# A recurrent attention and feed-forward kernel: inputs of three batches in half-batch loads from ScalarE's queue

## Chip, core and metric

One core of a Trainium2 chip runs the kernel. The engines are named as in the profile: PE (matrix multiplies; PEld is its weight load), DVE (vector), ACT (scalar and activation functions), POOL, and SP, which here only issues DMAs. Each engine works through its own instructions in program order and waits at the first one whose inputs or buffers are not ready. A DMA is issued by SP or ACT on that engine's queue. The metric is device time in microseconds of one execution, as a median over runs; details come from one profiled execution.

## What is computed

Four batches, eight heads, 768 steps, head size 48. A gated linear recurrence gives `y`; a feed-forward block with the gate `h * cos(h)` follows.

```python
for t in range(S):
    state = alpha[:, :, t, :, None] * state + np.einsum('bhd,bhe->bhde', k[:, :, t], v[:, :, t])
    y[:, :, t] = np.einsum('bhd,bhde->bhe', q[:, :, t], state)
x = y.transpose(0, 2, 1, 3).reshape(B * S, H * D)      # 3072 x 384
h = x @ w_in                                           # w_in 384 x 2048
g = h * np.cos(h)
out = g @ w_out                                        # w_out 2048 x 384
```

## The kernel before

The 3072 rows are cut into 24 chunks of 128 steps; chunk j belongs to batch j // 6 and holds all eight heads. In a chunk the recurrence is done as matrix products: cumulated logarithms of alpha give scale factors, k and q are scaled by them, k·q scores are masked, and a state is carried from chunk to chunk of a batch. The feed-forward block of a chunk has two halves of eight 128-column blocks.

The whole program is a hand-scheduled list: `ORDER` is a string of units, each a letter and a number, and every engine executes its instructions in the order in which the units stand there. The units that matter, with the engine:

- `a`, `k`, `q`, `v` + chunk: load of one input. In the kernel before SP issues one load of 192 KB for each chunk and tensor (lines 100 and 104), 96 in all. A row of one head is 48 floats, so each load is cut into 1024 pieces of 192 bytes. Buffers: six chunks for k, q, v (`PF`), four pairs of chunks for alpha.
- `z0`..`z3`, `Z0`..`Z3`: a quarter of `w_in` (line 111) or `w_out` (line 124), 768 KB each, from SP. `r`, `s` cast a quarter of `w_in` (DVE two thirds, ACT one third); `R` casts a quarter of `w_out` (DVE for even numbers, ACT for odd ones).
- `i`/`l`: logarithm of alpha on ACT for one or two chunks (line 144); `c`/`C`: cumulated sums on PE (lines 157, 161); `d`/`E`: two exponentials on ACT (lines 175, 177). Logarithm and exponential use one activation table and the cosine another, so ACT loads a table at each change (lines 137 and 338).
- `K`, `Q`: scaled k and q on POOL (lines 185, 191; `Q0` and `Q1` on DVE); `b`: cast of v on POOL (line 195); `E_`: a small factor on POOL (line 200).
- `T`: transpose of scaled k and q; on PE with a copy `t` by DVE (lines 218, 224) for chunks below `TD`, from there as a DMA transpose issued by SP (line 211).
- `A`, `m`: scores on PE, mask on DVE (lines 235, 244). `S`, `u`: state on PE and its update on DVE and POOL (lines 260, 272, 274). `Y`, `y`: outputs of the recurrence on PE, copied by DVE (lines 289, 292, 299). `D`: transpose of these into x, on PE with the DVE copy `B` for chunks below 6, from there as a DMA transpose from SP (line 307).
- `F`, `G`: first matrix product of the feed-forward, first and second half (line 330; 24 matmuls each). `f_`, `g_`: the cosine on ACT (line 338). `p`, `Q_`: the product on DVE (line 344). `V`, `W`: second matrix product (line 352; 8 matmuls each). `e`: ACT copies the result out of PSUM (line 357) and issues the store (line 358).
- `w` + n: n dummy matmuls, fillers where PE would stand still (line 368).

`V0` is the first second-product unit. All eight quarters of the weights are cast before or shortly after it: `V` uses the quarters `Z0` and `Z1`, `W` the quarters `Z2` and `Z3`, `F` uses `z0` and `z1`, `G` uses `z2` and `z3`.

Of the kernel before, what the change touches and what calls it, by code (L numbers as in the profile page):

```python
# [9 lines left out]
FP = mybir.dt.float32  # L10
BF = mybir.dt.bfloat16
AF = mybir.ActivationFunctionType
# [4 lines left out]
def kernel(  # L17
# [10 lines left out]
    nc = tc.nc  # L28
    B, H, S, D = q.shape
    DM, DF = moe_w_in.shape  # L30
    C = 128
    NC = S // C
    NCH = B * NC
    NP = H // 2
    NF = DF // C
    HF = NF // 2
    HD = H * D
    TD = 8
    QB = 6
    XD = 6  # L40
    CW = HD + NP
    ACOL = [(h % 2) * NP + h // 2 for h in range(H)]
    PF = 6

    consts = ctx.enter_context(tc.tile_pool(name="consts", bufs=1))
    apool = ctx.enter_context(tc.tile_pool(name="apool", bufs=4))
    inpool = ctx.enter_context(tc.tile_pool(name="inpool", bufs=PF))
    cpool = ctx.enter_context(tc.tile_pool(name="cpool", bufs=4))
    work = ctx.enter_context(tc.tile_pool(name="work", bufs=2))
    moe = ctx.enter_context(tc.tile_pool(name="moe", bufs=2))  # L50
    ps = ctx.enter_context(tc.tile_pool(name="ps", bufs=1, space=bass.MemoryType.PSUM))
# [13 lines left out]
    lnab = consts.tile([C, 2, 2, H, 64], BF, tag="lnab")  # L65
# [5 lines left out]
    khb, qhb = kqb[:, :, 0], kqb[:, :, 1]  # L71


    vpb = consts.tile([C, 3, H, D], BF, tag="vpb")
# [5 lines left out]
    m2 = consts.tile([C, 2], FP, tag="m2")  # L80
# [1 line left out]
    nc.vector.memset(m2[0:64, 0:1], 1.0)  # L82
    nc.vector.memset(m2[64:128, 1:2], 1.0)

    w1f = consts.tile([C, 3, DF], FP, tag="w1f")
    w1 = consts.tile([C, 3, DF], BF, tag="w1")
    w2f = consts.tile([C, NF, DM], FP, tag="w2f")
    w2 = consts.tile([C, NF, DM], BF, tag="w2")

    a_t, q_t, k_t, v_t, cp_t, icp_t = {}, {}, {}, {}, {}, {}  # L90

    def rows(t, j):
        b, c = j // NC, j % NC
        return t[b, :, c * C : (c + 1) * C, :].rearrange("h s d -> s h d")

    def load_a(j):
        if j % 2 == 0:
            a_new = apool.tile([C, 2, H, D], FP, tag="a_sb")
            a_t[j // 2] = a_new
        nc.sync.dma_start(out=a_t[j // 2][:, j % 2], in_=rows(alpha, j))  # L100

    def load(nm, src, d, j):
        t = inpool.tile([C, H, D], FP, tag=nm)
        nc.sync.dma_start(out=t, in_=rows(src, j))  # L104
        d[j] = t

    QF = DF // 4

    def load_w1(h):
        f = slice(h * QF, (h + 1) * QF)  # L110
        nc.sync.dma_start(out=w1f[:, :, f], in_=moe_w_in[:, f].rearrange("(k p) f -> p k f", p=C))  # L111

    def cast(eng, dst, src):
        if eng is nc.scalar:
            eng.activation(out=dst, in_=src, func=AF.Copy)
        else:
            eng.tensor_copy(out=dst, in_=src)

    def cast_w1(h, eng, k0, k1):
        f = slice(h * QF, (h + 1) * QF)  # L120
        cast(eng, w1[:, k0:k1, f], w1f[:, k0:k1, f])

    def load_w2(h):
        nc.sync.dma_start(  # L124
            out=w2f[:, 4 * h : 4 * h + 4],
            in_=moe_w_out[4 * h * C : (4 * h + 4) * C, :].rearrange("(f p) n -> p f n", p=C),
        )

    def cast_w2(h):
        cast((nc.vector, nc.scalar)[h % 2], w2[:, 4 * h : 4 * h + 4], w2f[:, 4 * h : 4 * h + 4])  # L130


    table = [None]
# [1 line left out]
    def lnset():  # L135
        if table[0] != "ln":
            nc.scalar.preload_act_table_set("natural_log_exp_and_others")  # L137
            table[0] = "ln"

    def ln(j0, n):  # L140
        lnset()
        g = j0 // 2
        lo = j0 % 2
        nc.scalar.activation(  # L144
            out=lnab[:, g % 2, lo : lo + n, :, 0:D], in_=a_t[g][:, lo : lo + n], func=AF.Ln
        )

    cum_ps = {}
# [33 lines left out]

    def khat(j):
        icp = icp_t[j // 2][:, j % 2]
        nc.gpsimd.tensor_tensor(out=khb[:, j % 3, :, 0:D], in0=k_t.pop(j),  # L185
                                in1=icp.rearrange("s (h d) -> s h d", h=H), op=ALU.mult)

    def qhat(j):
        cp = cp_t[j // 2][:, j % 2]
        eng = nc.vector if j < 2 else nc.gpsimd  # L190
        eng.tensor_tensor(out=qhb[:, j % 3, :, 0:D], in0=q_t.pop(j),  # L191
                          in1=cp[:, 0:HD].rearrange("s (h d) -> s h d", h=H), op=ALU.mult)

    def vcast(j):
        nc.gpsimd.tensor_copy(out=vpb[:, j % 3, :, 0:D], in_=v_t.pop(j))  # L195

    def emask(j):
        cp = cp_t[j // 2][:, j % 2]
# [9 lines left out]
    def transposes(j):  # L208
        if j >= TD:
            t = work.tile([C, 2 * NP, C], BF, tag="qkT", bufs=QB)  # L210
            nc.sync.dma_start_transpose(out=t, in_=kqb[:, j % 3].rearrange("s i h d -> s (i h d)"))  # L211
            qkT_t[j] = t.rearrange("r b s -> r (b s)")
            return
        t = ps.tile([C, 2 * NP * C], BF, tag="g")
        qkT_ps[j] = t
        for i, src in enumerate((khb, qhb)):
            for p in range(NP):
                nc.tensor.transpose(
                    t[:, (i * NP + p) * C : (i * NP + p + 1) * C],
                    src[:, j % 3, 2 * p : 2 * p + 2].rearrange("s h d -> s (h d)"), ident_bf)  # L220
# [141 lines left out]
    def warmup(n):  # L362
# [7 lines left out]

    dve, act_e = nc.vector, nc.scalar
    units = {
        "a": load_a, "k": lambda j: load("k_sb", k, k_t, j), "q": lambda j: load("q_sb", q, q_t, j),
        "v": lambda j: load("v_sb", v, v_t, j), "z": load_w1, "Z": load_w2,
        "r": lambda h: cast_w1(h, dve, 0, 2), "s": lambda h: cast_w1(h, act_e, 2, 3), "R": cast_w2,

        "i": lambda j: ln(j, 1), "c": lambda j: cums(j, 1), "d": lambda j: exps(j, 1),
# [37 lines left out]
    for u in ORDER.split():
        nm = u.rstrip("0123456789")
# [29 lines left out]
```

## Time and profile before

| | |
|---|---|
| three runs | 199.65, 200.43, 196.9 us (median 199.65) |
| the profiled execution | 197.87 us, of which 195.9 us from first to last instruction |
| busy: PE, DVE, ACT, POOL | 176.9, 123.6, 117.4, 75.4 us |
| granted PE clock | 1.00 throughout |
| first matmul, first `F`, first `V` | 5.5, 29.7, 47.3 us |
| dummy matmuls | 56 recorded, 16.3 us, all before 47 us |
| table loads on ACT | 16, 1.28 us each |
| HBM read, written | 25.17 MB, 4.72 MB |

Busy times of matmuls overlap each other, since PE is a pipeline: 24 matmuls of a unit `F` are listed with 219 ns each but follow each other every 56 ns. Where a sum needs PE's pace, it is read from the spacing, as the chain of waits lists it. "SPq" and "ACTq" are the queues' own instructions, DMA issues above all; their time is not in the busy time of an engine. The DMA share in the profile counts overlapping pieces and can exceed one; GB/s is what was moved.

### The profile page before, as it was taken

The page shows a single profiled execution, that of the slowest core. Times are in us where ns is not written, and L with a number is a line of the kernel's source. Part 1 is how long each engine was busy: PE and PEld are TensorE (multiplying, and loading weights), DVE is VectorE, ACT ScalarE, POOL GpSimd, SP SyncE. Part 2 cuts the span into 40 slices and gives each one's busy share as a digit, 9 for nine tenths or more (in the row PEclk, how much of TensorE's full clock was granted, in tenths as well). Part 3 has the DMA queues.
Part 4 walks back from the last instruction along what each step waited for, and adds up shares of the span by engine and source line. Part 5 has one row for each costly group of instructions (what it writes and reads, how often), then busy time and mean ns, then how long its engine had stood idle before and what let it go on. Part 6 is the DMA issues. An engine that isn't in the chain of part 4 may idle for free.

```text
span 195.9 us, 5535 instructions
## 1 busy us (share of the span) xinstructions
PE 176.9 (90%) x2338; PEld 133.6 (68%) x2342; DVE 123.6 (63%) x147; ACT 117.4 (60%) x133; POOL 75.4 (38%) x116
## 2 busy tenths in 40 slices
PE   0899889899999789999898998997998999999993
PEld 0355448698677578887577776776876976697761
DVE  6164767889827647768726585755973698376720
ACT  2344365577877586456686578796857834344641
POOL 4215654340268328252136471533548605220000
PEclk9999999999999999999999999999999999999999
DMA  6999999999999999999999999999899966913012
GB/s 122 191 187 188 240 264 289 324 348 232 209 228 216 210 169 195 179 174 208 234 173 182 163 239 175 187 173 218 156 196 196 221 143 129 182 45 76 7 40 80
DMA packets 131416, 36.20 MB, mean 185 GB/s; under 512 B 124736, under 2 KB 129856, under 8 KB 131392
## 3 DMA queue, kind: packets, MB, share of 16 engines
q1 hardware_dynamic: 127936, 31.14, 88.8%
q10 hardware_dynamic: 3456, 4.72, 9.3%
q8 instruction: 18, 0.29, 0.7%
q14 instruction: 6, 0.05, 0.1%
HBM read 25.17 MB, written 4.72 MB: 153 GB/s over the span
## 4 chain that ended last, share of the span: by engine, by line
PE 31%; SPq 24%; DMA 21%; DVE 7%; issue 7%; POOL 5%; ACT 3%; ACTq 0%; POOLq 0%; DVEq 0%
PE o_new L352 14%; PE t L330 13%; SPq L104 11%; SPq L100 5%; DMA x<-t 4%; DMA w2f<-in_moe_w_out_dram 4%; DVE g_new L344 4%; DMA t<-in_k_dram 4%; SPq L111 3%; SPq L124 3%; DMA t<-in_v_dram 3%; DMA t<-kqb 3%; DMA a_new<-in_alpha_dram 2%; POOL kqb L185 2%; SPq L211 1%
## 5 line engine op out<-in xcount | busy, mean ns | idle before, releaser
L330 PE MATMUL t<-x,w 128*128 128x128 bf16 x1152 | 70.6, 219 | 2.2 <-DMA x<-t 2.1
L344 DVE TENSOR_TENSOR g_new<-t,c_sb 128x1024 bf16<-128x1024 f32 x48 | 58.1, 1221 | 20.6 <-ACT c_sb L338 20.0
L338 ACT ACTIVATE c_sb<-t,halfpi 128x1024 bf16<-128x1024 f32 x48 | 53.0, 1112 | 29.4 <-PE t L330 26.6
L330 PEld LDWEIGHTS <-w 128*128 128x128 bf16 x1152 | 65.5, 98 | 5.0 <-DMA x<-t 2.4
L352 PE MATMUL o_new<-w,g_new 128*128 128x384 bf16 x384 | 68.8, 326 | 0.1
L352 PEld LDWEIGHTS <-g_new 128*128 128x128 bf16 x384 | 35.2, 97 | 20.2
L244 DVE TENSOR_TENSOR t<-t,mask_f 128x1024 bf16<-128x1024 f32 x24 | 28.7, 1218 | 5.3 <-PE t L235 5.3
L185 POOL TENSOR_TENSOR kqb<-t,icp_new 128x384 bf16<-128x384 f32 x24 | 23.9, 999 | 17.3 <-DMA t<-in_k_dram 15.3
L195 POOL CAST vpb<-t 128x384 bf16<-128x384 f32 x24 | 12.1, 503 | 37.4 <-DMA t<-in_v_dram 37.4
L274 POOL TENSOR_TENSOR ub<-sc,Em 128x384 bf16<-128x384 f32 x16 | 13.6, 852 | 28.9 <-DVE sc L272 28.9
L191 POOL TENSOR_TENSOR kqb<-t,cp_new 128x384 bf16<-128x384 f32 x22 | 21.9, 999 | 5.6 <-DMA t<-in_q_dram 3.0
L299 DVE CAST t<-t 128x384 bf16<-128x384 f32 x24 | 13.3, 553 | 14.3 <-PE t L292 14.2
L357 ACT ACTIVATE o_sb<-o_new 128x384 f32<-128x384 f32 x24 | 11.7, 486 | 17.4 <-PE o_new L352 17.4
L144 ACT ACTIVATE lnab<-a_new 128x768 bf16<-128x768 f32 (+1 forms) x13 | 10.3, 794 | 13.9 <-DMA a_new<-in_alpha_dram 13.9
L368 PE MATMUL w_new<-warm 128*128 128x512 bf16 x56 | 16.3, 410 | 0.2
L272 DVE TENSOR_TENSOR sc<-t,ub 128x384 f32<-128x384 f32 x16 | 8.8, 552 | 8.8 <-PE t L260 8.8
L157 PE MATMUL cum_new<-lnab,triu_bf 128*128 128x384 bf16 x24 | 7.5, 339 | 7.6 <-ACT lnab L144 7.6
L175 ACT ACTIVATE icp_new<-cum_new 128x768 f32<-128x768 f32 (+1 forms) x13 | 9.9, 759 | 5.5 <-PE cum_new L161 4.5
L292 PEld LDWEIGHTS <-t 128*128 128x128 bf16 x192 | 9.7, 96 | 3.9 <-DVE t L244 1.2
L292 PE MATMUL t<-vpb,t 128*128 128x48 bf16 x192 | 11.2, 184 | 0.8 <-DVE t L244 0.4
L137 ACT ACT_TABLE_LOAD x8 | 10.3, 1283 | 2.4 <-ACT o_sb L357 1.6
L161 PEld LDWEIGHTS <-lnab 128*128 128x128 bf16 x96 | 5.5, 98 | 8.6 <-issue 6.8
(43 smaller groups left out, 120.4 us busy)
## 6 DMA issues: line engine op xcount, KB each, us to landing
t<-in_v_dram SPq DMA_DIRECT2D x24, 192.0 KB, 4.6
a_new<-in_alpha_dram SPq DMA_DIRECT2D x24, 192.0 KB, 4.6
t<-in_k_dram SPq DMA_DIRECT2D x24, 192.0 KB, 4.4
t<-in_q_dram SPq DMA_DIRECT2D x24, 192.0 KB, 4.3
out_dram<-o_sb ACTq DMA_DIRECT2D x24, 192.0 KB, 3.3
w1f<-in_moe_w_in_dram SPq DMA_DIRECT2D x4, 768.0 KB, 7.0
w2f<-in_moe_w_out_dram SPq DMA_DIRECT2D x4, 768.0 KB, 9.2
x<-t SPq DMA_TRANSPOSE x18, 3.9
```

Source lines behind the costliest of these rows:

```text
L104: nc.sync.dma_start(out=t, in_=rows(src, j))
L185: nc.gpsimd.tensor_tensor(out=khb[:, j % 3, :, 0:D], in0=k_t.pop(j), in1=icp.rearrange("s (h d) -> s h d", h=H), op=ALU.mult)
L191: eng.tensor_tensor(out=qhb[:, j % 3, :, 0:D], in0=q_t.pop(j), in1=cp[:, 0:HD].rearrange("s (h d) -> s h d", h=H), op=ALU.mult)
L244: nc.vector.tensor_tensor(out=t.rearrange("s (h t) -> s h t", h=H), in0=A_ps.pop(j).rearrange("s (h t) -> s h t", h=H), in1=mask_f.unsquee ...
L274: eng.tensor_tensor(out=ub[:, us(j), :, 0:96].rearrange("r p (a e) -> r p a e", a=2), in0=sc.rearrange("r p (a e) -> r p a e", a=2), in1=E ...
L292: nc.tensor.matmul(t[:, h * D : (h + 1) * D], A_t[j][:, ACOL[h] * C : (ACOL[h] + 1) * C], vpb[:, j % 3, h], start=first, stop=True, skip_g ...
L299: nc.vector.tensor_copy(out=t, in_=y_ps.pop(j)[:, 0:HD])
L330: nc.tensor.matmul(t[:, f], w1[:, kk, ft * C : (ft + 1) * C], x_t[j][:, kk], start=(kk == 0), stop=(kk == 2))
L338: nc.scalar.activation(out=c_sb, in_=h_ps[j, half], func=AF.Sin, bias=halfpi, scale=1.0)
L344: nc.vector.tensor_tensor(out=g_new, in0=h_ps.pop((j, half)), in1=c_t.pop((j, half)), op=ALU.mult)
L352: nc.tensor.matmul(o_ps[j][:, 0:DM], g[:, f], w2[:, half * HF + f], start=(f == 0 and half == 0), stop=(f == HF - 1 and half == 1))
L368: nc.tensor.matmul(w_ps, warm[:, 0:C], warm, start=True, stop=True)
```

## The change

Batch 0 is still loaded chunk by chunk from SP. For batches 1 to 3 each tensor comes in two loads, of four heads and all six chunks each, that ACT issues: 24 loads of 576 KB (3072 pieces of 192 bytes). They stand in `ORDER` as chunks 6, 7 (batch 1), 12, 13 (batch 2) and 18, 19 (batch 3); the units of the other chunks of these batches are gone. A tile now holds one tensor of a batch, and there are two of them for each tensor. The float32 weights go through four shared buffers instead of having their own, so `Z1`, `Z0`, `Z3`, `Z2` each reuse the buffer of a quarter of `w_in` once it is cast. `TD` goes from 8 to 6, so `T6` and `T7` become DMA transposes. The buffers for the exponentials go from four to three. `ORDER` is new throughout; the number of dummy matmuls in it goes from 60 to 62, and the changes of ACT's table from 16 to 12.

```diff
-    TD = 8
+    TD = 6
...
-    apool = ctx.enter_context(tc.tile_pool(name="apool", bufs=4))
-    inpool = ctx.enter_context(tc.tile_pool(name="inpool", bufs=PF))
-    cpool = ctx.enter_context(tc.tile_pool(name="cpool", bufs=4))
+    inpool = ctx.enter_context(tc.tile_pool(name="inpool", bufs=2))
+    cpool = ctx.enter_context(tc.tile_pool(name="cpool", bufs=3))
...
+    def load(nm, src, j):
         b, c = j // NC, j % NC
+        if c == 0:
+            t_new = inpool.tile([C, H * NC, D], FP, tag=nm)
+            in_t[nm, b] = t_new
+        t = in_t[nm, b]
+        if b == 0:
+            nc.sync.dma_start(out=t.rearrange("p (h c) d -> p h c d", c=NC)[:, :, c],
+                              in_=src[b, :, c * C : (c + 1) * C, :].rearrange("h s d -> s h d"))
+        else:
+            hh = slice(c * (H // 2), (c + 1) * (H // 2))
+            nc.scalar.dma_start(out=t[:, hh.start * NC : hh.stop * NC],
+                               in_=src[b, hh].rearrange("h (c p) d -> p (h c) d", p=C))
...
     def load_w1(h):
         f = slice(h * QF, (h + 1) * QF)
-        nc.sync.dma_start(out=w1f[:, :, f], in_=moe_w_in[:, f].rearrange("(k p) f -> p k f", p=C))
+        t = inpool.tile([C, 3, QF], FP, tag="wf", bufs=4)
+        nc.sync.dma_start(out=t, in_=moe_w_in[:, f].rearrange("(k p) f -> p k f", p=C))
+        wf_t[h] = t
...
     def load_w2(h):
...
+        t = inpool.tile([C, 4, DM], FP, tag="wf", bufs=4)
...
     ORDER = (
...
+        "k0 q0 v0 b0 a0 a1 k1 q1 a2 a3 a4 v1 v2 a5 a6 a7 i0 i1 w11 c0 d0 E_0 k2 K0 w2 c1 d1 Q0 Q1 w7 T0 t0 w4 "
+        "A0 q2 q3 K1 b1 T1 v3 k3 q4 q5 l1 m0 C1 k4 k5 z0 k6 E1 K2 t1 z1 z2 k7 z3 w4 S0 u0 A1 w2 Y0 y0 m1 w3 "
+        "D0 B0 Q2 Q3 b2 l2 b3 w5 Y1 y1 C2 w1 D1 B1 l3 C3 E2 E3 S1 l4 l5 K3 E_1 u1 w3 T2 E_2 K4 t2 w4 A2 T3 t3 "
+        "Q4 v4 m2 v5 w4 S2 u2 C4 q6 C5 w1 T4 t4 q7 A3 m3 E_3 w2 Y2 y2 r0 E4 s0 E_4 E_6 K5 Q5 A4 b4 w2 S3 u3 "
+        "w3 D2 r1 E5 Z1 s1 m4 Z0 F0 f_0 v6 s2 B2 r2 T5 t5 p0 w4 A5 Z3 r3 Q6 Q7 Y3 y3 s3 G0 m5 Z2 v7 D3 B3 g_0 "
+        "G1 b5 S4 Q_0 u4 G2 G3 g_1 g_2 Y4 Q_1 Q_2 F1 y4 K6 K7 Q8 F2 T6 g_3 Q_3 a12 R1 D4 f_1 F3 b6 R0 B4 p1 "
+        "Y5 V0 y5 f_2 f_3 R2 F4 R3 K8 Q9 a13 p2 p3 f_4 T7 T8 D5 B5 p4 W0 e0 G4 g_4 V1 S6 b7 Q_4 K9 T9 u6 W1 "
+        "A6 A7 G5 m6 e1 Y6 y6 m7 V2 S7 D6 E_7 u7 g_5 Q_5 l6 W2 Y7 y7 D7 e2 l7 A8 K10 E_8 k12 b8 v12 C6 V3 W3 "
+        "m8 S8 F5 u8 Q10 Q11 E6 G6 e3 T10 Y8 y8 K11 T11 f_5 g_6 b9 D8 F6 f_6 V4 k13 p5 p6 W4 e4 S9 F7 f_7 E_9 "
+        "E_10 Q_6 u9 V5 W5 v13 q12 p7 A9 K12 A10 m9 E_12 m10 e5 G7 G8 g_7 Q_7 V6 g_8 Y9 y9 W6 l8 q13 Q_8 e6 "
+        "A11 C7 D9 m11 b10 S10 u10 F8 b11 K13 E7 Y10 V7 b12 y10 Y11 F9 G9 Q12 Q13 W7 y11 b13 Q14 D10 f_8 f_9 "
+        "p8 D11 p9 K14 S12 F10 a18 g_9 Q_9 e7 T12 G10 T13 F11 Q15 a19 f_10 g_10 K15 T14 T15 u12 S13 f_11 q18 "
+        "E_13 u13 p10 V8 W8 G11 Q_10 e8 g_11 p11 A12 m12 b14 V9 C8 Q_11 E8 Q16 Q17 E_14 S14 u14 W9 e9 Y12 y12 "
+        "E_15 D12 q19 A13 A14 l9 A15 k18 V10 m13 Y13 b15 m14 y13 W10 K16 m15 l10 k19 Y14 C9 E9 D13 e10 F12 "
+        "y14 Y15 y15 G12 S15 f_12 p12 g_12 Q_12 D14 b16 V11 W11 e11 F13 f_13 E_16 E_18 Q18 K17 G13 G14 K18 "
+        "v18 V12 g_13 p13 g_14 v19 Q_13 Q_14 T16 A16 W12 e12 F14 D15 m16 f_14 F15 u15 Y16 y16 f_15 V13 S16 "
...
```

## Prediction

> **What bounds the kernel now.** I read the page's busy times and chain of waits first.
>
> ```profile
> PE 176.9 (90%) x2338; PEld 133.6 (68%) x2342; DVE 123.6 (63%) x147; ACT 117.4 (60%) x133; POOL 75.4 (38%) x116
> PE 31%; SPq 24%; DMA 21%; DVE 7%; issue 7%; POOL 5%; ACT 3%; ACTq 0%; POOLq 0%; DVEq 0%
> ```
>
> PE is nearly always busy, yet the chain that ended last gives 45% to SP's DMA issues and to transfers. The chain in order of time shows where: to 46 us it is SP's issues and a weight transfer, afterwards mostly PE. PE's timeline marks the border, the first second-product unit (`V0`):
>
> ```profile
> 47.15 0.33 PE L260 MATMUL t<-vpb,kqb 128*128 128x96 bf16 x4
> 47.32 1.46 PE L352 MATMUL o_new<-w,g_new 128*128 128x384 bf16 x8
> ```
>
> The pace of PE's units stands in the chain, pipelined:
>
> ```profile
> 112.55 0.35 PE t L235 x8
> 179.34 4.02 PE t L330 x72
> 183.36 2.60 PE o_new L352 x16
> ```
>
> So `F`/`G` take 1.34 us, `V`/`W` 1.30, `A` 0.35; from the same view `C` (two chunks) 0.5, `Y` 0.40, `S` 0.17, `T` 0.45, `D` 0.17. After 47.3 us PE still has 48 × 1.30 + 39 × 1.34 + 19 × 0.35 + 8 × 0.5 + 19 × 0.40 + 15 × 0.17 + 2 × 0.45 + 0.2 = 136.5 us of work, and 195.9 − 47.3 = 148.6 us pass. Of the 12.1 us over, 3.4 are the last copy and store after the last matmul (192.5 to 195.9); some 8.7 are waits. So the kernel has a ramp of 47 us, PE work of 137 us, and waits of 9 us. These last come largely through POOL:
>
> ```profile
> POOL vpb L195 <- DMA t<-in_v_dram: 37.4, 12, 7.3
> POOL kqb L185 <- DMA t<-in_k_dram: 15.3, 10, 4.4
> ```
>
> The ramp is set by transfers. SP's timeline at the start (start, duration), a window table (last column GB/s), and SP's timeline at a moment when its queue was empty:
>
> ```profile
> 0.74 0.45 SPq L104 DMA_DIRECT2D t<-in_v_dram  x1
> 1.25 1.45 SPq L100 DMA_DIRECT2D a_new<-in_alpha_dram  x2
> 2.75 0.89 SPq L104 DMA_DIRECT2D t<-in_k_dram  x1
> 3.68 1.85 SPq L104 DMA_DIRECT2D t<-in_q_dram  x2
> 5.57 0.96 SPq L100 DMA_DIRECT2D a_new<-in_alpha_dram  x1
> ```
>
> ```profile
> 10.00:18.00 8.00, 7.87 (x72) 4.05 (x71) 4.55 (x7) 3.97 (x6) 3.45 (x4) 1.00 1.43 187
> 41.00:46.00 5.00, 5.00 (x99) 5.00 (x95) 4.45 (x6) 4.33 (x4) 1.00 (x1) 1.00 1.07 364
> ```
>
> ```profile
> 49.26 0.53 SPq L104 DMA_DIRECT2D t<-in_k_dram  x1
> 49.88 0.65 SPq L104 DMA_DIRECT2D t<-in_v_dram  x1
> 50.59 0.91 SPq L104 DMA_DIRECT2D t<-in_k_dram  x1
> ```
>
> Input loads move at a flat 187 GB/s, so 192 KB (0.197 MB) cost 1.05 us and SP is held at that pace after about three loads: the queue holds two to three loads, and a further issue stands until older pieces have left. Weights, in pieces of 1.5 to 2 KB, move at 364 GB/s, 2.16 us for 768 KB. The ramp before is full: the 25 loads and 8 weight quarters that SP issues up to `Z3` are 26.3 + 17.3 = 43.6 us, and the last of them lands at 46.2.
>
> **The change part by part.**
>
> *The ramp.* The bytes and the 192-byte pieces are the same; what changes is when they are asked for. Before `V0` the new order puts all of batch 0 (24 loads, SP) and, on ACT's queue, `a6 a7 k6 k7 q6 q7 v6 v7 a12`. `V0` needs `R1` on ACT, which stands behind the issues of `v7` and `a12`; since an issue stands while its queue is full, `v6` must be through by then. Moved before `V0`: 24 × 1.05 = 25.2; seven half-batch loads at 3 × 1.05 = 3.15, 22.1; `z0`–`z3` 8.6; `Z1`, `Z0` 4.3. That is 60.2 us, from the first moved bytes at 1.9 us (the DMA view of the first 20 us): `V0` at 62, 15 us later than now. The beginning shows it already: `a0` is SP's fourth load, and with `a6` taking half of the rate it lands at about 1.9 + 8 × 1.05 = 10.3 us, where the logarithm now starts at 4.96. PE cannot use the time: the units before `V0` are again chunks 0 to 5 and eight `F`/`G`; dummies and waiting fill it. Behind ACT's standing `k7` are the logarithms and `E2`, `E3`; behind `q7` are `s0` and `s1`, for which `F0` and the buffers of `Z1` and `Z0` wait (SP stands there too, with `T6` behind it). `E5` waits for POOL's `K5`, `Q5` (three buffers instead of four), which comes later than these loads only if POOL does; I cost it at nothing while ACT is held anyway, 1 to 2 us else. Bounds: 52 us, if an issue costs ACT only 0.7 us (0.45 us for 1024 pieces in SP's first row against 0.34 us for the store of 128 pieces below, so 0.11 for each further 896), and 68 us, if the two queues leave gaps while each waits for the other. I take 62, from the flat rate.
>
> A page of the Trainium skill speaks against the change: "DMA: Bandwidth & Descriptors", section "Issuing engines are not separate DMA queues", says that DMAs issued by several engines share the same 16 DMA engines and only the issuing time is saved. The flat 187 GB/s above comes from one queue alone, so no row here tests two. Its section "Rules for kernel authors" speaks for it, asking to join small transfers, and its table of measured sizes (138 GB/s at 64 KB, 341 at 1 MB) would put 576 KB at an estimated 300 GB/s: 2.0 us a load, 8 us off the ramp, 205 us in all. The rows have 192 KB loads at 187 and 768 KB loads at 364, but back to back and with pieces of different size; the change keeps the 192-byte piece, so I stay at 187.
>
> *ACT after `V0`.* Store issues are what ACT's queue shows now:
>
> ```profile
> 125.82 0.34 ACTq L358 DMA_DIRECT2D out_dram<-o_sb  x1
> ```
>
> From `R1` to `g_14` ACT has 24 cosines × 1.06 = 25.4, 12 copies and stores × 0.88 = 10.6, 5 logarithms × 0.84 = 4.2, 4 pairs of exponentials × 1.52 = 6.1, 6 table loads × 1.29 = 7.7, two casts of `w_out`, 3.0: together 57.0 us. In the same stretch stand 15 half-batch loads. One costs between 0.7 us (above) and 3.15 us (queue full); the nearest row is the three loads from an empty queue, 49.26 to 51.50 = 2.24 us, less two fixed parts of 0.34: 1.56 us. So 23.4 us, and ACT needs 80.4 us for a stretch in which PE has 70.5 us (`V0` to `G14`: 24 × 1.30 + 21 × 1.34 + 10 × 0.35 + 10 × 0.40 + 4 × 0.5 + 9 × 0.17 + 0.2). ACT sets this stage by 10 us; behind each issue stands the next cosine, for which DVE's product and then `V` or `W` wait. Bounds: at 0.7 us ACT needs 67.5 and PE sets the stage; at 3.15, 104 us. Their buffers are free long before (batch 2 needs batch 0 used up), so I put no other wait on them; if POOL lags by a chunk, ACT would stand 1 to 2 us at `k12` or `v12`.
>
> *What is gained.* POOL's waits for loads go, as each batch is in before it is used; this is most of the 8.7 us of waits. Four table loads fewer, 5.1 us of ACT, of which the stage above already has its share. `T6`, `T7` leave PE: 0.9 us; SP gets two more transposes (1.2 to 3.8 us of issue), with `A6` several units later, so nothing there. SP, freed of 72 loads, has only transposes later on.
>
> *The end.* After `G14`: 24 × 1.30 + 19 × 1.34 + 8 × 0.35 + 8 × 0.40 + 2 × 0.5 + 6 × 0.17 = 64.7 us, with no loads left, plus 3.4. Sum: 62.1 + 80.4 + 64.7 + 3.4 = 210.6 us, and with the 2.0 us that the profiled execution has around its span 212.6: 213. That execution (197.87) is 0.9% below the median of the three, so I leave the sum as it is.
>
> **Rivals.** (1) *ACT keeps up*: the ramp is as above, but an issue costs 1 us or less, so PE sets the rest with 5 us of waits: 62.1 + 135.2 + 5 + 3.4 + 2 = 208. For it: ACT is idle 29 of the 100 us from 50 to 150 now. (2) *ACT's issues return at once*, so `R1` and the casts are not held, and only the share of the rate delays the ramp: `V0` at 53, 4 us of waits: 198. Against: SP's rows from the third load on. (3) *Faster: two queues add up.* If 187 GB/s is the limit of one queue feeding small pieces and not of the transfers, SP and ACT together could come towards the 364 GB/s that the weights reach. Then 45 load-equivalents and six quarters are (8.8 + 4.7 MB) / 364 = 37 us, the ramp stays at 47.3, and with waits down to 2 us it is 47.3 + 135.2 + 2 + 3.4 + 2 = 190. It decides once both together pass about 270 GB/s, where `V0` comes at 52 (8.8 MB at 270 is 33, the weights 13, 2 for the start, some 4 for the casts) and the lost waits pay for it. For it: 364 GB/s is possible in the same transfers. Against: the DMA share of 1.43 at 187 GB/s, which says that pieces already lie in wait beside each other.
>
> **How the numbers follow.** Forecast 45%, with a range of its own of 205 to 224; rival 1 27%; rival 2 14%; rival 3 14%. Faster or slower means by over 2%, 195.7 and 203.6 us, about what three runs between 196.9 and 200.4 can tell. Slower is the forecast and rival 1, 72%; rival 2 is within, 14%; rival 3 is faster, 14%. The range of 8 in 10 leaves out most of rival 3 and the upper end of the ACT bound: 196 to 224.
>
> **What would show it.** The first logarithm near 10 us instead of 5; ACT's queue with issues of 1.5 to 6 us at `a7`, `k7`, `q7`, `v7`; GB/s flat near 187 while both queues are full; the first `F` past 40 us and the first `V` near 62; between 62 and 142 ACT without idle time and PE idle before `V`; POOL's wait for v and k near zero. A rate well above 187 with both queues active, or issues below 1 us on ACT, would make the prediction wrong.

## The result, and the profile after

The changed kernel takes 228.16 us (median of three runs, 227.57 to 228.76) against 199.65 us (196.9 to 200.43): a ratio of 1.151, 95% interval 1.131 to 1.171. The profiled execution took 228.76 us, 227.0 of it from first to last instruction. The direction was forecast; the size, 15 us beyond the forecast and 4 above the range, was not.

From the page of the changed kernel, the busy times, the granted clock in 40 slices, the rate in 40 slices, and the shares of the chain of waits:

```profile
PE 188.1 (83%) x2324; PEld 140.9 (62%) x2328; DVE 121.4 (54%) x145; ACT 111.6 (49%) x129; POOL 75.9 (33%) x116
...
PEclk9758985995967999999969997999999999999999
...
GB/s 126 174 197 186 184 177 209 340 292 248 314 281 191 173 119 110 195 210 196 217 100 127 193 208 115 202 182 203 198 57 109 90 98 147 36 54 55 56 35 69
...
PE 52%; ACTq 10%; SPq 10%; ACT 9%; issue 7%; DMA 5%; DVE 4%; POOL 2%; POOLq 0%; DVEq 0%
```

ACT's queue is new in the chain with a tenth of the span, and SP's share has halved. The clock is no longer full in the first third. The high rates, where the weights move, begin in the eighth slice. PE's timeline shows where `V0` is now (the line of eight matmuls at the end), and what comes just before it:

```profile
66.29 2.72 PE L331 MATMUL t<-x,w 128*128 128x128 bf16 x24 [5.26 <-DVE g_new L345]
...
69.47 3.30 PE L331 MATMUL t<-x,w 128*128 128x128 bf16 x48
...
72.78 1.50 PE L331 MATMUL t<-x,w 128*128 128x128 bf16 x24
...
74.49 1.46 PE L353 MATMUL o_new<-w,g_new 128*128 128x384 bf16 x8
```

`V0` comes at 74.5 us instead of 47.3. At that point both orders leave nearly the same work for PE: 136.5 us before and 135.2 after, counted by the units from `V0` on with the prediction's prices. Behind it pass 148.6 us before and 152.5 after. So of the 31.1 us between the two spans, 27.2 lie before `V0` and 3.9 behind it. The ramp is the question.

ACT's timeline of the ramp (start, duration, in brackets the idle time before and what ended it) shows the half-batch loads (L99) and what stands behind them:

```profile
0.74 4.19 ACTq L99 DMA_DIRECT2D t_new<-in_alpha_dram  x2
...
11.58 0.52 ACT L144 ACTIVATE lnab<-t_new 128x384 bf16<-128x384 f32 x1 [5.34 <-DMA t_new<-in_alpha_dram]
...
22.38 0.55 ACTq L99 DMA_DIRECT2D t_new<-in_k_dram  x1
...
36.58 10.68 ACTq L99 DMA_DIRECT2D t_new<-in_q_dram  x2
...
48.72 0.63 ACT L115 ACTIVATE w<-t 128x512 bf16<-128x512 f32 x1
...
55.54 8.28 ACTq L99 DMA_DIRECT2D t_new<-in_v_dram  x1
56.02 0.61 ACT L115 ACTIVATE w<-t 128x512 bf16<-128x512 f32 x1
63.86 3.12 ACT L339 ACTIVATE c_sb<-t,halfpi 128x1024 bf16<-128x1024 f32 x3 [7.22 <-issue]
```

With `a6` and `a7` in the queue from 0.74 us, the first logarithm comes at 11.58 us instead of 4.96; a run below, where these two are asked for later, has it at 7.63, so about 4 of the 6.6 us are theirs. `q6` and `q7` hold ACT for 10.7 us, `v7` for 8.3, and the three cosines that the next products and matmuls need come only when `v7` has gone out, at 63.86. Behind `q7` the cast `s0` ends at 49.35, and at 49.37 SP's timeline has the first quarter of `w_out`, which takes the buffer of the quarter that `s0` has read; before it was issued at 30.63:

```profile
49.37 13.51 SPq L125 DMA_DIRECT2D t<-in_moe_w_out_dram  x4
```

Window tables (window, length, busy time of PE, PEld, DVE, ACT, POOL, clock, DMA share, GB/s), of the changed kernel:

```profile
0.00:70.00 70.00, 44.86 (x428) 28.09 (x433) 28.84 (x45) 24.00 (x32) 23.56 (x41) 0.78 1.23 225
10.00:20.00 10.00, 5.12 (x28) 2.25 (x28) 1.12 (x2) 3.53 (x7) 3.13 (x4) 0.54 1.44 193
20.00:30.00 10.00, 9.73 (x114) 5.53 (x113) 6.50 (x10) 5.31 (x7) 1.50 (x2) 1.00 1.48 183
```

and of the kernel before:

```profile
0.00:70.00 70.00, 60.27 (x741) 41.77 (x746) 45.14 (x64) 40.61 (x49) 29.39 (x50) 1.00 1.14 232
```

In the first 70 us both kernels move nearly the same number of bytes, at 225 and 232 GB/s. What they buy differs: PE issues 428 matmuls instead of 741. And with both queues full the small pieces still move at 183 to 193 GB/s, against 187 from SP alone.

### The profile page after: what moved, and what is told of

Same layout as the page of the kernel before. It is cut to its first block, busy times and chain, and to the rows that moved or that the text cites. A ratio compares the mean times of both kernels' runs of the same rounds, so it can differ in the third digit from the quotient of the medians.

```text
span 227.0 us, 5441 instructions
## 1 busy us (share of the span) xinstructions
PE 188.1 (83%) x2324; PEld 140.9 (62%) x2328; DVE 121.4 (54%) x145; ACT 111.6 (49%) x129; POOL 75.9 (33%) x116
## 4 chain that ended last, share of the span: by engine, by line
PE 52%; ACTq 10%; SPq 10%; ACT 9%; issue 7%; DMA 5%; DVE 4%; POOL 2%; POOLq 0%; DVEq 0%
PE t L331 23%; PE o_new L353 19%; SPq L95 10%; ACTq L359 7%; DMA t_new<-in_q_dram 5%; ACT c_sb L339 4%; ACTq L99 3%; PE t L236 2%; ACT cp_new L178 2%; PE w_new L369 2%; DVE g_new L345 2%; PE t L293 2%; ACT o_sb L358 1%; PE t L290 1%; DVE t L245 1%
## 5 line engine op out<-in xcount | busy, mean ns | idle before, releaser
L331 PE MATMUL t<-x,w 128*128 128x128 bf16 x1152 | 73.5, 224 | 13.8 <-DVE g_new L345 8.0
L331 PEld LDWEIGHTS <-w 128*128 128x128 bf16 x1152 | 68.7, 100 | 16.5 <-issue 13.1
L353 PE MATMUL o_new<-w,g_new 128*128 128x384 bf16 x384 | 70.2, 332 | 0.0
L186 POOL TENSOR_TENSOR kqb<-t_new,icp_new 128x384 bf16<-128x384 f32 x24 | 25.0, 1047 | 21.9 <-DMA t_new<-in_k_dram 11.1
L192 POOL TENSOR_TENSOR kqb<-t_new,cp_new 128x384 bf16<-128x384 f32 x22 | 21.8, 1001 | 27.2 <-DMA t_new<-in_q_dram 12.7
L275 POOL TENSOR_TENSOR ub<-sc,Em 128x384 bf16<-128x384 f32 x16 | 13.3, 831 | 49.2 <-DVE sc L273 48.9
L369 PE MATMUL w_new<-warm 128*128 128x512 bf16 x58 | 21.6, 504 | 1.6 <-DVE warm L56 1.2
L196 POOL CAST vpb<-t_new 128x384 bf16<-128x384 f32 x24 | 12.8, 539 | 18.7 <-DMA t_new<-in_v_dram 18.7
L144 ACT ACTIVATE lnab<-t_new 128x768 bf16<-128x768 f32 (+1 forms) x13 | 10.1, 791 | 14.7 <-DMA t_new<-in_alpha_dram 11.0
L178 ACT ACTIVATE cp_new<-cum_new 128x776 f32<-128x776 f32 (+1 forms) x13 | 9.9, 763 | 6.6 <-POOL Em L201 6.6
L225 DVE COPY t<-t 128x1024 bf16<-128x1024 bf16 x6 | 4.1, 690 | 15.3 <-PE t L219 15.3
```

The costliest lines, as they stand in the source:

```text
L178: nc.scalar.activation(out=cp_t[g][:, lo : lo + n], in_=cum_ps[g][:, lo : lo + n, 0:CW], func=AF.Exp, scale=1.0)
L186: nc.gpsimd.tensor_tensor(out=khb[:, j % 3, :, 0:D], in0=inp("k", j), in1=icp.rearrange("s (h d) -> s h d", h=H), op=ALU.mult)
L192: eng.tensor_tensor(out=qhb[:, j % 3, :, 0:D], in0=inp("q", j), in1=cp[:, 0:HD].rearrange("s (h d) -> s h d", h=H), op=ALU.mult)
L331: nc.tensor.matmul(t[:, f], w1[:, kk, ft * C : (ft + 1) * C], x_t[j][:, kk], start=(kk == 0), stop=(kk == 2))
L353: nc.tensor.matmul(o_ps[j][:, 0:DM], g[:, f], w2[:, half * HF + f], start=(f == 0 and half == 0), stop=(f == HF - 1 and half == 1))
L369: nc.tensor.matmul(w_ps, warm[:, 0:C], warm, start=True, stop=True)
```

## The experiments

Two theories were tested. **A**: the loads cost time because their issues stand on ACT, with cosines, exponentials and casts behind them. **B**: they cost time because they ask for the bytes of batch 1 ahead of the weights; at the fixed rate of 192-byte pieces, 48 input loads and eight quarters need 48 × 1.05 + 8 × 2.16 + 1.9 = 69.6 us, on whichever queue they are. Theory C of the expectations puts the loss down to the new order itself and to the low clock; two sets of runs further down bear on it. The moments below come from PE's timelines; the landing of the last quarter of `w_out`, and how many input loads (in units of 192 KB) had landed by then, are counted in the trace's transfers. The last column is B's sum for that number of loads, so it tests the rate at which the bytes came, and not what `V0` waited for.

| kernel | time, us | first `F` | `V0` | span − `V0` | last weight in | loads by then | sum |
|---|---|---|---|---|---|---|---|
| before | 199.65 | 29.7 | 47.3 | 148.6 | 47.7 | 26.7 | 47.2 |
| changed | 228.16 | 48.9 | 74.5 | 152.5 | 67.7 | 46.1 | 67.6 |
| loads from SP | 233.83 | 38.4 | 64.1 | 167.9 | 69.3 | 45.3 | 66.7 |
| batch 1 from SP | 229.39 | 38.6 | 66.9 | 160.7 | 72.3 | 48.2 | 69.8 |
| later `a6 a7` | 229.34 | 46.8 | 75.6 | 152.0 | 66.6 | 44.9 | 66.3 |
| later `v` | 224.09 | 48.4 | 67.2 | 155.1 | 65.2 | 43.8 | 65.2 |
| later `q v` | 222.77 | 45.0 | 69.6 | 151.4 | 64.8 | 43.4 | 64.8 |
| long pieces | 205.03 | 39.0 | 57.0 | 146.3 | 59.5 | | |
| chunk loads, 25 ahead | 219.37 | 49.1 | 64.0 | 153.3 | 63.1 | 36.1 | 57.1 |
| chunk loads, 40 ahead | 213.32 | 41.0 | 57.1 | 154.1 | 60.9 | 37.2 | 58.2 |
| more dummies | 227.18 | 47.7 | 72.7 | 152.7 | 67.8 | 46.3 | 67.8 |
| stores from POOL | 225.86 | 48.5 | 74.8 | 149.3 | 68.0 | 45.8 | 67.3 |
| order before, early loads | 208.45 | 30.2 | 47.9 | 159.5 | 47.9 | 26.6 | 47.1 |
| order before, ACT's halves | 217.2 | 30.4 | 48.1 | 167.0 | 48.2 | 26.6 | 47.1 |

The kernel before took 200.15, 198.13, 197.66 and 198.65 us on the chips of these runs. Where no interval is given, a time is that of one run; as the kernel before differs by 2.5 us between these chips, differences of 2 to 3 us between total times are not read.

**All half-batch loads from SP.**

```diff
-            nc.scalar.dma_start(out=t[:, hh.start * NC : hh.stop * NC],
+            nc.sync.dma_start(out=t[:, hh.start * NC : hh.stop * NC],
```

> The 24 half-batch loads are issued by SP instead of ScalarE, at the same places of the order. Theory A (ScalarE is held by its own load issues, so logarithms, casts and cosines come late): ScalarE's queue has no long issues left, the first V starts at 62 to 66 us instead of 74.5 and the time falls to 214 to 219 us. Theory B (only the rate of 187 GB/s counts, whoever issues): the first V stays at 72 to 76 us and the time at 226 to 230. Theory C (the new order and the halved PE clock while it waits): 226 to 230 too, with the same clock of about 0.92.

No load stands on ACT any more, and `V0` comes 10.4 us earlier, as theory A had it. The time does not fall: 233.8 us, which neither theory forecast. PE's timeline shows where the 10 us went:

```profile
70.99 1.46 PE L353 MATMUL o_new<-w,g_new 128*128 128x384 bf16 x8 [2.91 <-DVE w L117]
...
82.79 0.61 PE L236 MATMUL t<-t 48*128 48x128 bf16 x8 [5.90 <-DMA t<-kqb]
```

and SP's timeline what set these two:

```profile
56.46 8.10 SPq L125 DMA_DIRECT2D t<-in_moe_w_out_dram  x2
64.61 0.50 SPq L99 DMA_DIRECT2D t_new<-in_v_dram  x1
65.20 6.35 SPq L212 DMA_TRANSPOSE t<-kqb  x1
```

`Z3` and `Z2` are held until 64.6 us and land at 69.3, so `W0` waits for a cast quarter; the first transpose of batch 1 stands 6.35 us behind the loads. The run carries a fault of its own, then: on SP the loads stand before transposes instead of cosines.

**Only batch 1 from SP**, the later batches from ACT, to keep that fault small.

```diff
+            eng = nc.sync if b == 1 else nc.scalar
-            nc.scalar.dma_start(out=t[:, hh.start * NC : hh.stop * NC],
+            eng.dma_start(out=t[:, hh.start * NC : hh.stop * NC],
```

> Only the eight half-batch loads of batch 1 go to SP, at their places; batches 2 and 3 stay with ScalarE. Theory A (in the ramp ScalarE's standing issues delay what stands behind them, after V0 it is another matter): V0 at 63 to 66 us as with all loads on SP, and from V0 on 150 to 154 us as in the changed kernel: 215 to 221 us. If the ramp's gain is given back later (the weights or the transposes behind SP's loads): V0 at 63 to 66, but 160 us or more after it, 225 us or more.

`V0` at 66.9, time 229.4, as the changed kernel: the second case of the expectation, the gain given back later. ACT is free in the ramp and waits for the weights themselves; in its timeline the cast of an odd quarter of `w_out`:

```profile
70.71 1.48 ACT L116 ACTIVATE w<-t 128x1536 bf16<-128x1536 f32 x1 [5.07 <-DMA t<-in_moe_w_out_dram]
```

PE's timeline has the same two waits as above behind `V0` (the lines are one further down here):

```profile
73.95 1.46 PE L354 MATMUL o_new<-w,g_new 128*128 128x384 bf16 x8 [1.77 <-DVE w L118]
...
82.93 0.61 PE L237 MATMUL t<-t 48*128 48x128 bf16 x8 [2.48 <-DMA t<-kqb]
```

Behind these lines POOL waits for the last load of batch 1, from POOL's timeline:

```profile
76.74 0.50 POOL L197 CAST vpb<-t_new 128x384 bf16<-128x384 f32 x1 [13.03 <-DMA t_new<-in_v_dram]
```

`V0` is 7.6 us ahead of the changed kernel, `W0` 3.4 us (73.95 against 77.30), since it waits for weights that land at 72.3 (B's sum says 69.8). The rest is lost by 90 us, with 3.0 us of waits for transposes, which still stand behind loads on SP, and some units at half clock. So freeing ACT in the ramp does not help by itself while the same loads are asked for ahead of the same weights; how much of the return is weights and how much SP's transposes, these two runs don't part cleanly.

**The same bytes in long pieces.** Each half-batch load reads its memory in one run of 4.6 KB for each partition. The tiles hold other rows by this, so the numbers computed are not the reference's; bytes, queues and order are those of the changed kernel.

```diff
-                               in_=src[b, hh].rearrange("h (c p) d -> p (h c) d", p=C))
+                               in_=src[b, hh].rearrange("h s d -> (h s d)").rearrange("(p x d) -> p x d", p=C, d=D))
```

> The half-batch loads keep their bytes, tiles and places but read each partition's 4608 bytes from one contiguous stretch of memory (the rows are then those of other steps and heads, so the output is not the reference's). 128 pieces instead of 3072. Theories A and B both put the cost down to 192-byte pieces, which fill a queue and move at 187 GB/s: issues of 0.4 us on ScalarE throughout, 1.6 us of transfer instead of 3.15, the first V at 56 to 62 us, 208 to 216 us. Theory C (order and clock): 224 us or more.

At 205.0 us it is 23 us faster than the changed kernel, more than the expectation gave: `V0` at 57.0, and 6.2 us less behind it. In ACT's timeline nothing stands any more, neither in pairs nor behind batch 0:

```profile
0.74 0.91 ACTq L99 DMA_DIRECT2D t_new<-in_alpha_dram  x2
...
29.92 0.82 ACTq L99 DMA_DIRECT2D t_new<-in_q_dram  x2
...
45.08 0.34 ACTq L99 DMA_DIRECT2D t_new<-in_v_dram  x1
```

All 24 issues take 9.6 us instead of 43.4, the stores 8.4 instead of 21.4, and the first 70 us move 252 GB/s instead of 225. The long issues are thus an effect of small pieces in a full queue, not of the size of a load. This run takes away both what stands on ACT and part of what the bytes cost, so it does not part A from B. With the two runs before it, it says that both count: in the changed kernel ACT's standing issues end the ramp, and some microseconds below lies the bound by the bytes, which is met as soon as ACT is free.

**The loads of batch 1 asked for later.** First `v6` and `v7` behind `R1`:

```diff
- ... F0 f_0 v6 s2 B2 ... G0 m5 Z2 v7 D3 B3 ... a12 R1 D4 ...
+ ... F0 f_0 s2 B2 ... G0 m5 Z2 D3 B3 ... a12 R1 v6 v7 D4 ...
```

> v6 and v7 move from behind f_0 and s3 to behind R1, so that no cosine g_0 to g_3 and no cast stands behind v7's issue. Theory A (the end of the ramp is ScalarE's work queued behind v7's standing issue, 10.7 us from its release at 63.8 to V0 at 74.5): V0 comes at 64 to 68 us; f_1 and the first chunks of batch 1 are later, so the time falls by less, to 219 to 225 us. Theory B (bytes that must pass before V0): V0 moves only by what v6 and v7 transfer, 2 x 3.15 us at most and less if the weights are last anyway: 70 us or later, 226 to 229 us.

then also `q6` and `q7` behind `s1`:

```diff
- ... S2 u2 C4 q6 C5 w1 T4 t4 q7 A3 ... E5 Z1 s1 m4 ... R1 D4 ...
+ ... S2 u2 C4 C5 w1 T4 t4 A3 ... E5 Z1 s1 q6 q7 m4 ... R1 v6 v7 D4 ...
```

> Beside v6 and v7 (behind R1), q6 and q7 move too, from before s0 to behind s1. Theory A (what ends the ramp is ScalarE's work behind its own standing issues): the casts s0 and s1 come at 36 to 40 us instead of 49 to 51, the first F at 38 to 42, V0 at 59 to 64 us, the time 216 to 223. Theory B (bytes that must pass): V0 stays at 66 to 69 us, where moving v6 and v7 alone left it, 223 to 226 us.

`V0` comes 7.3 and 4.9 us earlier, the time falls by 4.1 and 5.4. The first agrees with theory A in `V0` and in time, though 2.6 us of its gain are lost behind `V0`. The second does not: its first `F` (45.0) and its `V0` (69.6) are later than A said. There `q6` and `q7` stand again, now ahead of a cast of `w_in`, and POOL, ahead of `V0`, waits for their bytes; from the timelines of ACT, PE and POOL:

```profile
43.53 7.11 ACTq L99 DMA_DIRECT2D t_new<-in_q_dram  x2
```

```profile
53.65 2.81 PE L331 MATMUL t<-x,w 128*128 128x128 bf16 x22 [4.41 <-ACT w L115]
```

```profile
65.95 1.95 POOL L192 TENSOR_TENSOR kqb<-t_new,cp_new 128x384 bf16<-128x384 f32 x2 [13.54 <-DMA t_new<-in_q_dram]
```

Taking the loads from these places is thus worth some 5 us of the 28. That is no measure of all that standing issues cost, for moving a load along the same queue moves its stand with it.

**The start.** `a6` and `a7` go behind `d1` and `l1`, so that batch 0 has the transfers to itself at first.

```diff
- ... v2 a5 a6 a7 i0 i1 w11 c0 d0 E_0 k2 K0 w2 c1 d1 Q0 ... l1 m0 ...
+ ... v2 a5 i0 i1 w11 c0 d0 E_0 k2 K0 w2 c1 d1 a6 Q0 ... l1 a7 m0 ...
```

> Only a6 and a7 move: from the front of ScalarE's program to behind d1 and l1. The first logarithm should come at 6 to 9 us instead of 11.6. Theory A with a late start that carries through: the first V comes 5 to 6 us earlier, 221 to 224 us. Theory B (the same bytes have to pass before V0 anyway): the first V moves by less than 2 us, 226 to 229 us.

The first logarithm comes at 7.63 us and the first `F` 2.1 us earlier, `V0` not, as the expectation's theory B said. The late first logarithm is thus not what sets `V0`; ACT's queue stands at the loads that follow instead (`k6` for 4.9 us at 14.7).

**Chunk loads in the new order.** All inputs from SP again, 192 KB each, a fixed number of units ahead of their first use: first 25,

```diff
-        if b == 0:
+        if True:
...
- ... v2 a5 a6 a7 i0 ... z0 k6 E1 K2 t1 z1 z2 k7 z3 w4 ...
+ ... v2 a5 i0 ... z0 E1 K2 t1 z1 a6 a7 z2 z3 w4 S0 u0 a8 a9 ...
```

> The new order and everything else stays, but batches 1 to 3 are loaded chunk by chunk from SP again, each load 25 units ahead of its first use. Theories A and B (early, bulky loads): the first V comes at 46 to 52 us and the time is 196 to 206 us. Theory C (the new order itself is slow): 215 us or more.

then 40, with the alphas of batch 1 in two groups ahead of the weights, since this order takes the logarithms of chunks 6 to 11 early.

```diff
- ... K1 b1 T1 v3 k3 q4 q5 l1 m0 C1 k4 k5 z0 ...
+ ... K1 b1 T1 v3 k3 q4 q5 a6 a7 a8 a9 l1 m0 C1 k4 k5 a10 a11 z0 ...
```

> As the earlier chunk-wise run (new order, all loads from SP chunk by chunk), but its starved logarithms are mended: alpha of chunks 6 to 11 stands where a6 and a7 are needed, the other loads 40 units ahead of their use. If the form and the early place of the loads are the whole loss: V0 at 47 to 52 us, 197 to 204 us. If the new order has a share of its own (alpha and all of batch 0 ahead of the weights): V0 at 54 to 60 us, 204 to 212 us.

The first was starved: its logarithm of chunks 6 and 7 waited 14.9 us for alpha, the pair standing behind quarters of weights, so that its time, in the range of theory C, decides nothing. The second has `V0` at 57.1, like the run with long pieces, at 213.3 us, a microsecond above the range given for a share of the order. Two different ways of making batch 1 cheap in the ramp end at the same 57 us. In both, the last quarter of `w_in` lands at 43 to 44 us (36.8 in the kernel before), and from 46 or 47 us on the `F`/`G` that are left follow one another up to `V0` nearly without a wait. So most of the 10 us that remain to 47.3 belong to the order, which has all of batch 0 and six alphas ahead of the weights: 1.9 + 30 × 1.05 + 8.6 = 42.0 us for their last byte and a first `F` at 41.0, where the order before starts at 29.7 with part of batch 0 and of the weights. What this run loses behind `V0` is waiting for a cast and for a transpose, in PE's timeline:

```profile
62.79 1.46 PE L353 MATMUL o_new<-w,g_new 128*128 128x384 bf16 x8 [2.74 <-DVE w L117]
...
74.09 0.61 PE L236 MATMUL t<-t 48*128 48x128 bf16 x8 [5.40 <-DMA t<-kqb]
```

**The clock.** 86 more dummy matmuls where PE stood still.

```diff
- ... i1 w11 c0 ... K0 w2 c1 ... u1 w3 T2 ... Z0 F0 ... G2 G3 ...
+ ... i1 w34 c0 ... K0 w12 c1 ... u1 w18 T2 ... Z0 w14 F0 ... G2 w24 G3 ...
```

> More dummy matmuls where PE stood still in the ramp (w11 to w34, w2 to w12 before c1, w3 to w18 before T2, w14 before F0, w24 before G3: 86 more), so that the granted clock should stay at 1.00 up to V0. Theory C (the halved clock makes the ramp late): V0 at 69 to 71 us, 222 to 225 us in all. Theories A and B (the clock is a consequence of the waits): V0 at 73 to 76, 226 to 229 us.

The mean clock goes from 0.917 to 0.962 and `V0` comes 1.8 us earlier, between what theory C and the others said; the time, 227.18 us, can't be told from the changed kernel's 227.57 to 228.76. The page's clock line:

```profile
PEclk9999979998899999999969996799999999999999
```

Up to `V0` the stretches at a clock of 0.5 shrink from 30.7 to 6.8 us in the traces, so there the low clock costs some 2 us. Behind `V0` the low stretches stayed (6.8 and 10.2 us), and what they cost was not tested.

**The stores from POOL**, to see what of ACT's stage is due to them.

```diff
-        nc.scalar.dma_start(out=out[
+        nc.gpsimd.dma_start(out=out[
```

> The 24 stores are issued by GpSimd instead of ScalarE. Theory A (after V0 ScalarE is held by its queue: 19.9 us for loads, and 13.1 us more than before for stores that stand behind them): from the first V to the end 141 to 147 us instead of 152.5, 216 to 223 us in all. Theory B (transfers late, not ScalarE held): 226 to 229 us; GpSimd's own issues may add up to 3 us.

In the changed kernel a store behind a half-batch load stands with it, as in this stretch of ACT's timeline:

```profile
127.45 2.52 ACTq L99 DMA_DIRECT2D t_new<-in_q_dram  x1
...
130.74 4.54 ACTq L359 DMA_DIRECT2D out_dram<-o_sb  x1
135.38 1.11 ACT L339 ACTIVATE c_sb<-t,halfpi 128x1024 bf16<-128x1024 f32 x1 [4.67 <-PE o_new L353]
```

Together the stores take 21.4 us there, 8.3 in the kernel before. With the stores on POOL the stage from `V0` to `G14` shortens from 81.9 to 77.1 us; behind `V0` pass 149.3 us, more than theory A's 147, and the whole is 2.3 us shorter, which one run can hardly tell. The rest of the standing comes back elsewhere: the loads behind `V0` take 25.3 us instead of 19.9, and POOL pays for the stores, in its row of the page:

```profile
L359 POOL DMA_DIRECT2D out_dram<-o_sb x24 | 13.8, 576 | 61.1 <-ACT o_sb L358 61.1
```

**The order before with parts of the change**, in search of a version better than both. `TD` is 8 in these two, as before. First its chunk loads from SP some 20 units earlier, with the new tiles and pools:

```diff
- ... t5 g_3 Z0 R0 F3 Z3 G4 S4 V0 Q_3 f_3 A5 ...
+ ... t5 g_3 Z0 R0 F3 Z3 v5 v6 a8 a9 G4 S4 V0 Q_3 f_3 A5 k6 ...
```

> The program order of the kernel before and its chunk-wise loads from SP, with the tiles of the changed kernel (a batch per tile, shared weight buffers, three buffers for exponentials), and the loads that follow Z3 about 20 units earlier. If GpSimd's waits for loads are what the steady part of the kernel before loses (8.7 us of waits after V0), they go: 191 to 196 us. If loads are held by SP's transposes and the flat rate anyway, 197 to 203 us.

then with batches 2 and 3 in half-batch loads from ACT, one at a time behind a store or a cosine:

```diff
-        if b == 0:
+        if b < 2:
...
+ ... p3 g_4 Q_4 a8 a9 e0 a12 l4 F4 V1 W1 e1 a13 ... Q7 e2 k12 T7 ...
```

> The order of the kernel before; batches 0 and 1 chunk-wise from SP as there; batches 2 and 3 in half-batch loads from ScalarE, but one at a time, some 5 us apart, each behind a store. Theory A (the form costs only where two loads, or a load and a store, meet in ScalarE's queue, and where it comes before the weights): ScalarE's issues mostly 0.4 us, 193 to 200 us. Theory that half-batch loads of 192-byte pieces cost by themselves, wherever they stand: 205 us or more.

Both have `V0` at 48, as the kernel before, so the new tiles, the shared weight buffers and the third buffer less do not delay `V0` by themselves. Both are slower: 1.054 of its time (interval 1.048 to 1.060) and 1.092 (1.080 to 1.105). The first is beyond both of its forecasts, the second as slow as the theory that half-batch loads cost wherever they stand. In the first PE now waits for transposes of k and q, where the kernel before waits 0.7 us; from its list of waits (total, times, longest; the weight load and the matmul largely wait through the same time):

```profile
PEld L236 <- DMA t<-kqb: 13.3, 6, 5.5
...
PE t L236 <- DMA t<-kqb: 11.9, 6, 5.5
```

Earlier loads also stand in SP's queue ahead of transposes, though here tiles and pools changed too, so this is not pinned on the loads alone. In the second an issue by itself costs ACT next to nothing:

```profile
68.92 0.40 ACTq L99 DMA_DIRECT2D t_new<-in_k_dram  x1
74.18 0.45 ACTq L99 DMA_DIRECT2D t_new<-in_k_dram  x1
80.86 0.45 ACTq L99 DMA_DIRECT2D t_new<-in_q_dram  x1
```

and all 16 take 11.5 us, 4.9 of it at one place, where two follow each other at once. But the transposes beside them take longer to land. From its DMA view of 48 to 150 us (kind, number, median us from issue to landing):

```profile
x<-t SPq DMA_TRANSPOSE x10, 6.3
t<-kqb SPq DMA_TRANSPOSE x9, 6.4
```

and from the same view of the kernel before:

```profile
x<-t SPq DMA_TRANSPOSE x13, 4.4
t<-kqb SPq DMA_TRANSPOSE x12, 4.4
```

In the changed kernel, in the same window, transposes of k and q take 6.7 us and those into x 3.9, so the half-batch loads are not shown to be the cause. That they cost nothing once their issues are spaced is not borne out. How much of the 19 us in this run is transposes and how much POOL's wait for q (17.7 us in its list) was not separated. No kernel tried beat the one before.

## Why the prediction was right, and where it failed

Against the profiled execution the sum of 212.6 us is 16.2 short: the ramp by 12.4 (74.5 instead of 62.1), ACT's stage by 1.5 (81.9 for 80.4), what follows by 2.5 (70.6 for 64.7 + 3.4), the time around the span 0.2 less than put in.

**The step that failed is the ramp's end**, "seven half-batch loads at 3 × 1.05 = 3.15, 22.1; `z0`–`z3` 8.6; `Z1`, `Z0` 4.3", together with "PE cannot use the time: the units before `V0` are again chunks 0 to 5 and eight `F`/`G`". The direction, the rate and the mechanism held: small pieces fill the queue, the issuing engine stands, and the ramp grows. Its moment was even close: ACT came free of `v7` at 63.8 us. But it made the end of the transfers the start of `V0`, as if the eight `F`/`G` were done by then. Half of them (`G3`, `F1` to `F3`) and three cosines still stood behind `v7`, and they take the 10.7 us from 63.8 to 74.5, the first ones at half clock. A second omission hides beneath this one: `v7`, `Z3` and `Z2`, 3.15 + 4.3 = 7.5 us of transfers, were left out because they come after `V0`'s own inputs, though `W0` and the next chunk need them a few microseconds later. With them the sum is 69.6, and the last weight landed at 67.7, the 48th load at 70.4. In the changed kernel `W0`, at 77.3, no longer waits for them. The runs with loads on SP meet this second bound: they start `V0` 8 to 10 us earlier, and `W0` then waits for weights until 71 to 74 us.

- *Rate.* Right. With the loads that had in fact landed, the prediction's prices give the last weight's landing within 0.7 us in the kernel before and wherever ACT issues batch 1 in small pieces, 0.8 and 1.1 us early in the two runs with the order before, and 2.5 to 6.0 us early where SP issues batch 1 in the new order. One reading was off: 46.2 us, taken for the landing of the last weight before, is that of `Z0`; the last lands at 47.7.
- *Rival 3, two queues add up.* Refuted by 183 to 193 GB/s with both full. The Trainium skill, "DMA: Bandwidth & Descriptors", section "Issuing engines are not separate DMA queues", says the same; the advice of its section "Rules for kernel authors" to join small transfers did not help here, where the pieces stayed at 192 bytes, and the long pieces of one run did. The 300 GB/s that the prediction estimated for 576 KB from the page's table were not reached: small pieces moved at 193 GB/s at most in the windows above.
- *The start.* First logarithm forecast at 10.3, seen at 11.6; in the run with later `a6` and `a7` it comes at 7.6, and `V0` no earlier.
- *Issues on ACT.* "1.56 us a load" is right for none: alone a load costs 0.4 to 0.55 us, in succession up to 10 us a pair. The 23.4 us for 15 loads came out as 19.9 for the 14 behind `V0`, and the 13.1 us by which the stores grew were not foreseen. The stage's length agrees, its composition does not, so the agreement is luck.
- *POOL's waits go.* They do, but PE has nothing of it. In the changed kernel POOL's long waits for v and q end before `V0`; behind it POOL waits for a load once, for k, where the kernel before waits for loads there for some 42 us in all. From POOL's timeline of the changed kernel:

```profile
62.56 1.94 POOL L192 TENSOR_TENSOR kqb<-t_new,cp_new 128x384 bf16<-128x384 f32 x2 [8.69 <-DMA t_new<-in_q_dram]
...
155.27 1.00 POOL L186 TENSOR_TENSOR kqb<-t_new,icp_new 128x384 bf16<-128x384 f32 x1 [5.02 <-DMA t_new<-in_k_dram]
```

The prediction took these waits of POOL for most of PE's 8.7 us. PE itself waits for POOL for only 2.3 us in the kernel before, as its groups from 49.2 us on say (at the end of each line the idle time before it, and for what):

```profile
L289 PE MATMUL t<-ub,t 128*128 128x96 bf16 x64 | 7.9, 204 | 1.1 <-POOL ub L274 1.1
...
L260 PE MATMUL t<-vpb,kqb 128*128 128x96 bf16 x60 | 5.0, 206 | 1.2 <-POOL vpb L195 1.2
```

Behind `V0` the span of the changed kernel exceeds PE's work and the last store by 13.9 us (152.5 − 135.2 − 3.4), where it was 8.7. 6.2 us of this go with long pieces, which leaves 146.3 us behind `V0` against 148.6 before.

- *Rivals 1 and 2.* Both rest on cheap issues. Spaced out, issues are cheap, as rival 1 had it, but in this order they follow one another.

In sum, of the 28 us that the kernel lost, 23 go when the same loads have long pieces: 17.5 before `V0`, where the small ones are asked for ahead of the weights and hold ACT, and 6.2 behind it. How the 17.5 divide between the standing issues and the transfers is shown only in part: 5 us go with a few loads moved, and freeing ACT without shortening the transfers gains nothing in all. The 5 us left are put down to the order's later weights, 10 us at `V0`, of which a part is made good behind it; that follows from the two runs with `V0` at 57, and no run changed the order alone. The kernel before was not tried with long pieces, so what they would bring there stays open.

## What to carry to other kernels

When loads are moved ahead, list all that has been asked for before each thing that is waited for, on every queue together, and divide by the measured rate of pieces of that size: that sum gives the earliest landing, and it must run to the last transfer that the next units need, not to the first. Then ask what work still stands behind the last issue. Making a load larger without making its pieces longer did not make it faster here; it turned many short holds into a few long ones and passed them to whatever shares the queue.

## What was not expected of the hardware

A full queue holds whoever issues next, not only the large load: a store of 128 pieces, 0.34 us by itself, took up to 4.5 us behind a half-batch load.

The granted clock fell to 0.5 in the changed kernel in stretches of 3.4, 6.8 and 10.2 us, from 9.0, 32.9, 50.0 and 63.6 us on and twice later; in the 3.4 us ahead of each PE had been busy for 0.3 to 1.7 us. At the low clock 24 matmuls of an `F` took 2.7 us instead of 1.5. The Trainium skill, "TensorE: Matmul & The Clock Gate", part "The HAM clock gate", gives half rate after an idle window of about 3.4 us, which these multiples agree with, though PE was not wholly idle in the windows before.

In the run with the order before and spaced half-batch loads DMA transposes landed in 6.3 us instead of 4.4, at about the same rate of bytes (182 and 193 GB/s from 48 to 150 us). Why is not shown.
